# A hand-ordered plan for attention and channel mix on one core: every step in another place

## The chip, the core and the metric

The kernel runs on one core of a Trainium2 chip. A core has a matrix engine (TensorE, "PE" in the profile, with its weight loads as "PEld"), a vector engine (VectorE, "DVE"), a scalar engine (ScalarE, "ACT"), a general engine (GpSimd, "POOL") and a queue engine (SyncE, "SP"). Each runs its own list of instructions in order; they meet through semaphores. DMA transfers are issued from the lists of SyncE, ScalarE and GpSimd and share 16 DMA engines. Matmul results go to PSUM, which has eight banks. The metric is device time in microseconds (us) of one execution.

## The reference

Eight batches of 576 tokens, eight heads of 64 columns, 32 memory slots a head. Attention first squeezes keys and values into the memory slots, then each token attends to the 32 slots; a channel mix follows on the 512 columns.

```
a    = softmax over tokens of phi                  # per batch, head
k_m  = a^T k ;  v_m = a^T v                        # 32 x 64 per head
attn = softmax(q k_m^T / 8) over the 32 slots
x    = attn v_m                                    # heads side by side: 576 x 512
xk   = mu_k x + (1 - mu_k) x_prev ;  xr likewise with mu_r    # x_prev: the token before
out  = sigmoid(xr w_r) * (relu(xk w_k)^2 w_v)
```

The inputs and the output are float32.

## The kernel before

The work is cut into several hundred small steps. A text, `PLAN`, names them one after the other, and the loop at the kernel's end (L801) runs through its words and issues the instructions of each. Since every engine takes its instructions in that order, `PLAN` is the order of the work on each engine, and a semaphore wait on one engine holds all that stands behind it there.

A word is `who:name`, with marks behind it. `/a` has the step's copy or scaling done by ScalarE, `/d` by VectorE. `@` and digits name the PSUM banks that its matmuls write. A step whose matmuls are read later comes as two or three words: the first issues the matmuls, the next the reading. `who` is:

- a batch number, for attention: `exp` (exponentials of phi, L292), `z` (their sums and a reciprocal, L322 and L326), `k`, `v`, `kv` (slot means of keys and values, L312), `nk`, `nv` (dividing them), `tk` (turning the key means), `q0`, `q1` (turning q on VectorE, L381), `s` (scores, L395), `es` (their exponentials), `fe`, `fs`, `fo` (sums over the slots, by a turn, a reduction and a turn back on VectorE, L435 to L447), `w0`, `w1` (dividing, L458), `vt`, `vm` (turning the value means and mixing them with mu), `d` (differences of neighbouring tokens' weights). `G` and `E` multiply the value means into w_k and w_r and copy the products (L492, L498), `D` subtracts two of these (L501).
- `cN`, batch N's keys: `c2:5` is the sixth block of 128 columns of the hidden layer. Two matmuls with the weights, then a copy of that bank into a second one, then four matmuls with the differences, two in each (L617, L621, L625). `r` is the relu, `s` the square.
- `g` and `t`, the gate; `x` a gathering of leftover rows; `o` the product with w_v, with the gate applied and the store issued (L760, L771, L745).
- `p`, a load issued on GpSimd's queue: `p:v:1` is v of batch 1 (L181), `p:wk:2-4` a block of 256 columns of w_k (L208), `p:phi:4` L177.
- `b:NxM`, N matmuls of M times 64 columns on zeros whose result nobody reads (L259). A first group, `WARM = (10, 8)`, stands ahead of the plan.
- `w:03`, the store of a finished output tile that was held (the tiles in `HOLD`).

Batch 0 goes another way than the rest. It starts before most weights are there, so its q comes in two parts (`q:0a`, `q:0b`), as do its v, its scores (`s0`, `s1`), exponentials (`es00` to `es11`), denominators (`l`, `r`) and weights (`y`). `h` divides its key means. It mixes value means into whole token rows (`nk0`, `nr0` and so on here scale by mu, `mk`, `mr` are matmuls, L355, and `uk`, `ur` copies, L545) and then runs plain matmuls with w_k and w_r (`c0:3b`, L599; `g:00`, L666). `a` behind a key block is the first 256 tokens, `b` the other 320; `mk0` prepares `a`, `mk1` `b`. In batch 0's outputs `o:02a` and `o:02b` are column halves.

Loads on GpSimd's queue wait for two things: the buffer that they fill (two of each kind, so that batch 2 follows batch 0), and the load eight places ahead of them, whose semaphore they use again.

The stores of the last tile are cut in two: `o:71a` (352 columns) goes on ScalarE's queue and `o:71b` (160 columns) on SyncE's (`WHOLE`).

## Time and profile before

| | us |
|---|---|
| median of 3 runs | 189.69 |
| lowest, highest run | 189.14, 190.38 |
| span of the profiled execution | 187.8 |
| TensorE busy | 181.2 |
| VectorE busy | 153.9 |
| ScalarE busy | 151.9 |

The profile comes from one execution. Its page gives the span from first to last instruction, 187.8 us, and no other time for it; the median run stands 1.9 us above. "Busy" is the time in which an engine ran at least one instruction. TensorE's matmuls overlap and their ends are modelled, so the distance between the starts of two groups tells more of what a group costs than its own length. The "granted clock" is the share of full speed that the matrix engine was given. A DMA share over 1 means that several packets were in each DMA engine at once.

### The profile page before, as it was taken

How to read it: one execution, taken by the hardware profiler on the slowest of the kernel's cores; microseconds unless marked ns; L12 is line 12 of the kernel's file. 1: busy time of each engine (PE TensorE's matmuls, PEld its weight loads, DVE VectorE, ACT ScalarE, POOL GpSimd, SP SyncE). 2: the span in 40 equal slices, each digit the busy share in tenths (PEclk: the TensorE clock that was granted, in tenths of full speed). 3: DMA queues.
4: the chain of work that ended last, by engine and by line, in shares of the span. 5: the costliest groups of instructions: out<-in, count | busy, mean ns of one | idle time of the engine just before them, and what ended most of it. 6: DMA issues, size and time to landing. Idle time of an engine off the chain costs nothing.

```text
span 187.8 us, 6010 instructions
## 1 busy us (share of the span) xinstructions
PE 181.2 (96%) x2483; PEld 103.2 (55%) x2483; DVE 153.9 (82%) x328; ACT 151.9 (81%) x368; POOL 30.2 (16%) x46
## 2 busy tenths in 40 slices
PE   7979999999999999999999999999999999999992
PEld 2544566677644575556544655556545653465441
DVE  2334574899989999999999899999989999889441
ACT  2537889889999999999999889958999678775900
POOL 5943531060303040140032000000000010000000
PEclk9999999999999999999999999999999999999999
DMA  5999999999999999899989995114202224242054
GB/s 188 280 203 220 251 207 205 266 208 234 308 208 210 275 292 255 160 220 224 223 163 237 234 278 197 28 59 113 56 0 59 58 59 113 56 108 63 0 139 140
DMA packets 24923, 31.91 MB, mean 170 GB/s; under 512 B 1880, under 2 KB 19040, under 8 KB 24896
## 3 DMA queue, kind: packets, MB, share of 16 engines
q0 software_dynamic: 17936, 20.45, 59.0%
q1 hardware_dynamic: 5664, 9.00, 17.2%
q10 hardware_dynamic: 1296, 2.08, 3.3%
q8 instruction: 19, 0.31, 0.7%
q14 instruction: 8, 0.07, 0.1%
HBM read 38.28 MB, written 9.44 MB: 254 GB/s over the span
## 4 chain that ended last, share of the span: by engine, by line
PE 90%; DMA 4%; DVE 2%; issue 1%; ACT 1%; POOL 0%; POOLq 0%; DVEq 0%
PE pv L760 34%; PE pk L617 8%; PE pk L625 8%; PE pb L625 7%; PE gps L492 6%; PE pk L599 4%; DMA q<-in_q_dram 4%; PE pr L687 3%; PE pb L687 3%; PE pr L679 3%; PE kvps L312 3%; PE pr L709 2%; PE pr L666 2%; PE scps L395 2%; PE idle L259 1%
## 5 line engine op out<-in xcount | busy, mean ns | idle before, releaser
L760 PE MATMUL pv<-wv,sq 128*128 128x512 bf16 (+3 forms) x296 | 60.5, 350 | 0.0
L760 PEld LDWEIGHTS <-sq 128*128 128x128 bf16 x296 | 27.7, 98 | 24.9 <-issue 2.8
L498 ACT CAST G<-gps 128x512 bf16<-128x512 f32 x67 | 36.2, 629 | 1.2 <-PE gps L492 1.2
L771 DVE SCALAR_TENSOR_TENSOR o<-sg,pv 128x512 f32<-128x512 f32 (+3 forms) x41 | 24.9, 613 | 7.5 <-PE pv L760 5.1
L625 PEld LDWEIGHTS <-G 128*128 128x128 bf16 x224 | 21.4, 98 | 8.5 <-issue 0.7
L583 ACT ACTIVATE rl<-pk 128x288 bf16<-128x288 f32 (+2 forms) x49 | 20.0, 420 | 4.5 <-PE pk L625 3.9
L625 PE MATMUL pk<-diff,G 128*128 128x288 bf16 x112 | 22.9, 286 | 0.0
L625 PE MATMUL pb<-diff,G 128*128 128x288 bf16 x112 | 22.9, 286 | 0.0
L617 PE MATMUL pk<-atn,G 128*128 128x288 bf16 x112 | 20.8, 287 | 0.0
L621 ACT COPY pb<-pk 128x288 f32<-128x288 f32 x41 | 16.4, 410 | 5.1 <-PE pk L617 3.5
L591 DVE TENSOR_TENSOR sq<-rl 128x576 bf16<-128x576 bf16 (+2 forms) x46 | 18.3, 420 | 1.0 <-ACT rl L583 0.5
L583 ACT ACTIVATE rl<-pb 128x288 bf16<-128x288 f32 x40 | 16.2, 427 | 2.2 <-PE pb L625 1.8
L589 ACT ACTIVATE sq<-rl 128x576 bf16<-128x576 bf16 (+2 forms) x26 | 15.7, 624 | 0.5 <-DVE rl L585 0.4
L501 DVE TENSOR_TENSOR G<-G 128x1024 bf16<-128x1024 bf16 x21 | 14.3, 679 | 1.3 <-ACT G L498 1.3
L458 DVE TENSOR_TENSOR atn<-e,lz 128x576 bf16<-128x576 bf16 (+2 forms) x18 | 12.1, 683 | 3.5 <-ACT lz L430 3.5
L617 PEld LDWEIGHTS <-G 128*128 128x128 bf16 x112 | 10.2, 98 | 6.6 <-issue 1.5
L656 ACT ACTIVATE sg<-pr 128x512 f32<-128x512 f32 x22 | 13.0, 618 | 0.7 <-PE pr L687 0.6
L259 PE MATMUL idle<-zeros 128*128 128x512 bf16 (+3 forms) x47 | 12.2, 408 | 1.0 <-DVE zeros L187 1.0
L381 DVE STREAM_TRANSPOSE qT<-q 128x576 uint32<-128x576 uint32 (+2 forms) x16 | 12.1, 765 | 1.2 <-DMA q<-in_q_dram 1.2
L585 DVE TENSOR_SCALAR rl<-pk 128x288 bf16<-128x288 f32 (+2 forms) x23 | 10.1, 449 | 2.8 <-PE pk L599 2.6
L498 DVE CAST G<-gps 128x512 bf16<-128x512 f32 x17 | 11.3, 679 | 0.2 <-PE gps L492 0.2
L292 ACT ACTIVATE em<-ph 128x1152 bf16<-128x1152 f32 (+1 forms) x9 | 9.9, 1095 | 1.6 <-DMA ph<-in_phi_dram 1.6
(101 smaller groups left out, 283.7 us busy)
## 6 DMA issues: line engine op xcount, KB each, us to landing
out_dram<-o SPq DMA_DIRECT2D x46, 128.0 KB, 2.4
ph<-in_phi_dram POOLq DMA_DIRECT2D x7, 576.0 KB, 12.2
q<-in_q_dram POOLq DMA_DIRECT2D x7, 576.0 KB, 13.6
kv<-in_k_dram POOLq DMA_DIRECT2D x7, 576.0 KB, 14.2
kv<-in_v_dram POOLq DMA_DIRECT2D x7, 576.0 KB, 15.0
out_dram<-o SPq DMA_DIRECT2D x6, 256.0 KB, 6.5
out_dram<-o SPq DMA_DIRECT2D x20, 64.0 KB, 2.5
k0f<-in_k_dram ACTq DMA_DIRECT2D x2, 576.0 KB, 5.8
```

The source lines that it names most:

```text
L259: nc.tensor.matmul(ps.rearrange("p (a b) -> p a b", b=64), lhsT=zeros, rhs=zeros[:, :64].unsqueeze(1).to_broadcast([128, blocks, 64]), sta ...
L498: return lambda: copier()(g_tile()[:, v, c, GCOLS[i]], st["gps", v, i][c])
L501: return lambda: nc.vector.tensor_sub(g_tile()[:, 1, :, GCOLS[i]], g_tile()[:, 2, :, GCOLS[i]], g_tile()[:, 0, :, GCOLS[i]])
L583: nc.scalar.activation(rl, ps, AF.Relu, scale=HALF ** 0.5)
L589: nc.scalar.activation(dst, rl, AF.Square)
L591: nc.vector.tensor_mul(dst, rl, rl)
L617: nc.tensor.matmul(pa, lhsT=st["G"][:, 2, c, f], rhs=st["at"][:, c, :NP], start=c == 0, stop=False, skip_group_check=True)
L621: copier()(pb, pa)
L625: nc.tensor.matmul(ps, lhsT=st["G"][:, v, c, f], rhs=st["d"][:, kind, c], start=False, stop=c == 1, skip_group_check=True)
L656: nc.scalar.activation(gated[name], ps, AF.Tanh, scale=0.5)
L760: nc.tensor.matmul(pv[:, cols], lhsT=squares, rhs=wv_sb[:, fi, cols], start=(fi == 0), stop=(fi == NF - 1))
L771: nc.vector.scalar_tensor_tensor(o[:, cols], in0=gated[name][:, cols], scalar=1.0, in1=pv[:, cols], op0=AL.add, op1=AL.mult)
```

## The change

`PLAN` alone changes. All steps of real work are in both plans, each once; their order, the engine marks and the banks differ. The places that the later sections speak of:

- The unread matmuls. Behind `WARM`, the old plan has 37 in seven words ahead of the first key block. The new one has 22 in seventeen words, most of them ahead of `0:kg1`, and one more (`b:1x8`) ahead of `g:00`.
- The start of batch 0. `0:z`'s reciprocal and the two `0:h` stand ahead of `0:q0`, and both `0:h` are on VectorE. `0:vg1` and `0:vg0` stand ahead of the denominators `0:l11` and `0:l01`. `0:mk0` and `0:mr0` and the first 256 tokens' key blocks come first, where the old plan begins with `0:mk1` and the other 320 tokens.
- Loads. `p:wk:2-4` goes ahead of `p:wk:4-8`; `p:wv:0-2` ahead of `p:phi:2`; from there on q, k, v and phi of the later batches are in another order.
- `o:03b` stands ahead of `1:v`.
- The held stores `w:03`, `w:02`, `w:13`, `w:00`, `w:01` stand in the key stages of batches 1 and 2 instead of 3 and 4.
- The sums of batch 3 (`3:fe 3:fs 3:fo 3:w0`) stand close together on VectorE.
- The last words are `o:71b` and then `o:71a`.

```
 PLAN = [
-    "p:q:0b 0:c01/d 0:exp1 p:v:0h 0:c00/a 0:exp0 b:11x6@5 0:mub@0 0:mub 0:kg0@12 0:c10/d 0:c11/a b:2x8@5 0:kg1",
-    "0:z@0 0:q0 0:z 0:h1/a p:v:0g 0:h0/a b:7x7@5 0:tk@3 0:tk 0:q1 b:2x6@5 0:s0@1204 0:s1@3567 0:es00 0:es10",
-    "0:l00@1 0:l00 b:1x4@0 0:l10@2 0:l10 0:r00 0:y00 0:r10 0:y10 0:es01 0:es11 b:9x8@0 0:l11@4 0:l01@7 0:l01",
-    "0:r01 0:vg1@65 0:vg0 0:y01 0:nk0 0:l11 0:nk1 0:r11 0:y11 b:5x7@0 0:mk1@7321 0:uk11/a p:wk:4-8 0:mu@4",
-    "p:wk:2-4 0:uk10/d c0:3b@0 c0:4b@2 0:tb p:wk:0-2 c0:1b@1 c0:1b/d 0:nr1 c0:3b/a c0:3b/d p:phi:1 c0:0b@7 0:nr0",
...
-    "1:fe 1:fs g:02@4 g:03@6 g:01 g:03 o:02b@0 g:00@6 x:0/a c0:6a/d g:02 1:v@23 o:03b@5 1:fo 1:nv/a 1:vt@3 1:vm",
...
-    "c2:2 r:200/a r:201/a c2:4/a@1 3:tk r:220/d 4:q0 3:s@4035 r:221/a 3:es1 3:es0 p:v:4 c2:3@6 c2:3/d@7 s:20/d",
-    "c2:4 r:240/a c2:1@3 c2:7@5 c2:3 c2:1/a@0 4:q1 r:230/a g:20@4 s:22/d c2:7/a@2 r:231/a c2:1 r:211/a c2:5@6",
-    "r:241/a c2:5/a@7 c2:7 r:271/a 2:D2 3:fe 3:fs s:23/a r:270/a o:11@0 r:210/a o:11 g:20/a@1 c2:5 c2:6@3 3:vt@5",
...
-    "r:330/d s:31/d c3:0@4 c3:4 s:32/a s:35/a s:36/d g:30@6 o:23 w:03 w:00 g:31@7 c3:0/a@1 g:31/d@0 p:k:6 c3:0",
...
-    "s:76/a g:71/d@5 g:71 r:720/d s:72/d t:700 t:710 g:e3 t:711 r:730/d s:73/d x:7/a o:70@1 o:70 o:73@2 o:e3@1",
-    "o:73 t:701 o:e3 o:72@2 o:72 o:71a@0 o:71a o:71b@4 o:71b",
+    "0:exp0 b:1x4@3 0:mu@6 0:mu b:1x2@4 0:exp1 b:1x2@5 b:1x4@2 0:mub@2 b:2x8@7 0:z@1 b:1x8@5 0:c11/a b:2x8@4 b:1x8@4",
+    "0:c00/d 0:c01/d b:1x4@0 b:1x8@5 b:1x8@3 b:1x2@0 0:c10/d 0:z 0:kg0@34 0:kg1 b:2x8@0 b:2x8@5 0:h0/d 0:h1/d b:1x8@7",
+    "0:q0 0:tk@4 0:tk 0:s0@5310 0:es00 0:l00@6 0:es10 b:1x4@7 0:l00 0:r00 0:l10@5 0:l10 0:r10 p:q:0b 0:q1 p:v:0h",
+    "0:mub 0:s1@2763 0:es01 0:es11 p:v:0g 0:vg1@04 0:vg0 0:l11@3 0:l11 0:l01@6 0:l01 0:r01 0:r11 0:y00 0:y10 0:nk1",
+    "0:nk0 0:mk0@2157 b:2x8@3 0:nr1 0:nr0 0:uk01/d 0:y01 0:y11 0:mr0@7310 0:ur01/d p:wk:2-4 0:uk00/a c0:2a@6 c0:3a@4",
+    "c0:3a/d c0:3a/d p:wk:4-8 0:ur00/a 0:mk1@2573 p:wk:0-2 0:uk10/a p:phi:1 p:q:1 0:uk11/d c0:7a@0 c0:7a/a c0:7a/a",
...
+    "1:tk@4 1:tk 1:s@6521 1:es0 1:es1 1:fe 1:fs b:1x8@4 g:00@4 g:00 g:03@7 g:03 g:02@5 g:02 o:02b@2 g:01@6 o:03b@4",
+    "1:fo 1:w1 1:v@15 o:03b 1:w0 o:00b@3 o:02b g:01 x:0/a 1:nv/a 1:vt@7 1:vt/d 1:vm o:00b o:01b@6 o:01b 1:G00@45",
...
+    "c1:7@5 c1:4@0 r:101/a s:12/d r:100/d o:03a w:03 c1:7/a@1 c1:5 c1:7 r:170/d r:150/d c1:4/a@7 r:151/d 1:D2 3:exp",
...
+    "o:12@1 o:12 2:Es10/a 2:E000/a g:10/a@0 g:10 w:02 w:13 w:00 3:z@2 p:phi:4 4:exp 2:D0 w:01 t:100 t:101 2:G01@14",
...
+    "c2:0/a@4 3:tk@1 3:tk 2:D2 o:10@2 c2:0 r:200/a r:201/a o:10 c2:2 r:221/d 4:q1 c2:4@6 r:220/a c2:4/a@2 3:s@7451",
+    "3:es1 c2:3@0 c2:3/d@3 c2:4 r:241/d 3:es0 p:q:5 p:v:5 s:20/d 3:fe s:22/d 3:fs 4:q0 p:q:6 p:k:5 r:240/a s:24/d",
+    "3:fo 3:w0 c2:1@5 c2:1/a@2 c2:7@1 c2:7/a@6 c2:3 r:231/a r:230/a 4:z@7 c2:5@4 c2:5/a@3 c2:1 r:210/a c2:7 r:270/a",
...
+    "s:73/d s:71/a s:77/d s:70/a x:7/d o:62@2 o:62 g:70@1 g:70/d@4 o:70@7 g:70 t:701 g:71 t:700 o:70 o:73@3 g:e3@6",
+    "o:e3@2 t:710 t:711 o:73 g:e3 o:e3 o:72@1 o:72 o:71b@3 o:71b o:71a@5 o:71a",
 ]
```

## The prediction

> **What bounds the kernel now.** I read the page first, then stages, TensorE in order of time, and the loads that its first 40 us wait for.

> ```profile
> span 187.8 us, 6010 instructions
> PE 181.2 (96%) x2483; PEld 103.2 (55%) x2483; DVE 153.9 (82%) x328; ACT 151.9 (81%) x368; POOL 30.2 (16%) x46
> ```

> TensorE is busy for all but 6.6 us of the span. The stages (stretch, length, busy time of PE, PEld, DVE, ACT, POOL with instruction counts, granted clock, DMA share, GB/s) say where it isn't, and what runs beside it. The first two rows are of the same stretch, the second counts the unread matmuls alone:

> ```profile
> 12.00:15.40 3.40, 2.99 (x77) 1.47 (x75) 1.29 (x3) 2.48 (x9) 1.49 (x3) 1.00 1.22 206
> ```

> ```profile
> 12.00:15.40 3.40, 2.02 (x10) 0.87 (x9) 1.00 1.22 206
> ```

> ```profile
> 45.00:60.00 15.00, 15.00 (x237) 8.69 (x234) 14.25 (x33) 14.76 (x36) 2.98 (x4) 1.00 1.18 247
> 60.00:80.00 20.00, 20.00 (x326) 11.66 (x325) 19.57 (x37) 19.94 (x53) 2.98 (x4) 1.00 1.08 243
> ```

> From 45 us on TensorE has no free time, with VectorE and ScalarE close behind it. Ahead of that much of its work is filler (2.02 of 2.99 us in the first stretch). So a new order can gain in three places only: before the dense stretch starts, in small bubbles inside it, and after its end. TensorE's timeline (start, length, instruction) gives the edges:

> ```profile
> 0.99 4.38 PE L259 MATMUL idle<-zeros 128*128 128x512 bf16 x10 [0.99 <-DVE zeros L187]
> ```

> ```profile
> 19.75 3.54 PE L599 MATMUL pk<-x0T,wk 128*128 128x320 bf16 x24 [0.45 <-DVE x0T L545]
> ```

> ```profile
> 33.78 1.04 PE L760 MATMUL pv<-wv,sq 128*128 128x256 bf16 x8
> 34.66 1.03 PE L666 MATMUL pr<-wr,x0T 128*128 128x512 bf16 x4
> 35.61 0.75 PE L312 MATMUL kvps<-kv,em 64*32 64x64 bf16 x72
> ```

> The first key matmul starts at 19.75 us; the row at 35.61 is the step 1:v, batch 1's v means. Its data come over GpSimd's queue (issue row, then the DMA view of that moment, whose last number is us from issue to landing):

> ```profile
> 17.38 0.75 POOL L181 DMA_DIRECT2D kv<-in_v_dram  x1 [1.42 <-DMA wk<-in_moe_w_k_dram]
> ```

> ```profile
> kv<-in_v_dram POOLq DMA_DIRECT2D x1, 576.0 KB, 18.1
> ```

> 17.38 + 18.1 = 35.5 us: 1:v starts 0.1 us after its data are there. No wait shows, but nothing may come earlier either. The DMA engines are full throughout (share over 1), so this load is paced by what is queued ahead of it.

> **The start.** The chain that ended last begins with the first half of q (start, length, work):

> ```profile
> 3.08 7.02 DMA q<-in_q_dram
> 10.12 0.84 DVE qT L381
> 11.06 0.63 ACT kbd L337 x2
> ```

> ```profile
> 12.06 0.30 DVE kmT L365
> 12.40 0.53 PE scps L395 x30
> ```

> q lands at 10.10 in both plans, since GpSimd's queue begins alike. In the old plan VectorE turns q (0:q0) ahead of the reciprocal 0:z, so the key means are normalised (kbd, 11.06) only after the turn, and the scores wait until 12.40. The new plan puts 0:z and both normalisations (0:h0/d, 0:h1/d) on VectorE ahead of 0:q0; when the turn ends, at 10.12 + 0.84 = 10.96, only the 0.30 copy kmT is left. Scores start at about 11.35: 1.05 us earlier. The next stop is v's second half of batch 0, for 0:vg0, which now stands ahead of the denominators 0:l11 and 0:l01:

> ```profile
> 15.08 0.88 POOL L208 DMA_DIRECT2D wv<-in_moe_w_v_dram  x1 [1.22 <-DMA kv<-in_v_dram]
> ```

> ```profile
> 16.06 0.38 PE L420 MATMUL zps<-e,sumh 128*128 128x256 bf16 x2
> ```

> GpSimd's row shows that half landing just before 15.08, so the denominators come at about 15.2 instead of 16.06, 0.85 us earlier, and with them the first key: 18.9 us. It may be up to 1 us less, because the new plan starts with the first 256 tokens (0:mk0, c0:2a), which need the first half of the attention weights alone (0:y00, 0:y10, not 0:y01, 0:y11); I take 18.9, the later one. The column block of wk that these need is moved to the front of the wk loads (p:wk:2-4 ahead of p:wk:4-8), so that it doesn't bound them.

> **What the start is worth.** Counted word by word, everything that TensorE does ahead of 1:v in the old plan is ahead of it in the new one, and one thing more: o:03b, 8 matmuls of 256 columns, which cost 34.66 - 33.78 = 0.88 us. From first key to 1:v the old plan takes 35.61 - 19.75 = 15.86 us. The new one adds 0.88, a filler of 512 columns (about 0.2, an eighth of the 1.73 us of a value step below), and swaps mixing steps across the first key, 0:mk0 and 0:mr0 going ahead of it and 0:mk1 coming behind (two tile groups leave and one comes, of which I count no gain). It would be at 1:v at 18.9 + 15.86 + 1.1 = 35.85 with the late key, at 34.9 with the early one; about 35.5 between. The load says 35.5 too, and can't be beaten: GpSimd's order up to p:v:1 has the same loads. TensorE works in order, so o:00b, 1:vt and 1:G00 behind 1:v wait with it, whatever was won before. So 1:v comes 0.1 us earlier, with 0.88 us less left to do: a gain of 0.95 us, of which the late key would take 0.35.

> **The middle.** Behind 1:v both plans hold the same matmuls. Changes between full-array and tiled matmuls, which leave small gaps, number 27 groups behind the first key in the old plan and 26 in the new one, the one missing having moved ahead of it: no term. By the /a and /d marks some fifteen short copies (0:h, 0:ur, vt, nv) go from ScalarE to VectorE and a few back; TensorE's work hides them while neither engine falls behind. I cost the middle at nothing; a bubble that is new is a rival below.

> **The end.** The last output tile's columns are stored in two parts, 352 and 160 wide, and their order is swapped: the wide one is now last.

> ```profile
> L771 DVE SCALAR_TENSOR_TENSOR o<-sg,pv 128x352 f32<-128x352 f32 x1 | 0.5, 521 | 0.6 <-PE pv L760 0.6
> ```

> ```profile
> L771 DVE SCALAR_TENSOR_TENSOR o<-sg,pv 128x160 f32<-128x160 f32 x1 | 0.3, 320 | 0.0
> ```

> ```profile
> out_dram<-o ACTq DMA_DIRECT2D x1, 176.0 KB, 2.3
> ```

> ```profile
> out_dram<-o SPq DMA_DIRECT2D x1, 80.0 KB, 2.3
> ```

> After TensorE's last matmul the product takes 521 instead of 320 ns; both stores land 2.3 us after issue, and ScalarE's queue is as free as SyncE's. Loss: 0.2 us. A gain is excluded, since the wider product follows the same last matmul; if the wide product were hidden in part, the loss would go towards 0. I take +0.2, the rows' own difference.

> **The sum.** -0.95 + 0.2 = -0.75 us on the profiled span of 187.8, so 187.1. The span is the only time that the page gives; the median of the runs, 189.69, lies 1.9 above it, and I carry that over: **188.9 us**.

> **Rivals.** *Bubbles go too.* TensorE's weight loads stood idle for want of instructions, by the waits:

> ```profile
> PEld L492 <- issue: 4.4, 15, 0.4
> ```

> Nearly all of this lay under running matmuls (TensorE is 15.00 of 15.00 us busy), and the new plan has as many such groups in as long runs; if a quarter of the 4.4 us is exposed and all of it vanishes, 1.1 us, the time is 187.8. Chance 0.08.

> *The clock falls.* The first ten matmuls took 4.38 us, 0.43 each; eight of the same width later take 1.73 us, 0.22 each (the value step below). The granted clock reads 1.00 with TensorE 2.99 of 3.40 us busy; the new plan leaves 0.1 to 0.5 us of the 2.02 us of fillers there, so it would be busy for some 1.3 of 3.4 us, and no row shows that the clock stands it. If it drops for one phase as long as the first, 4.4 us, half of that, 2.2 us, is lost, 1:v comes at 37.7 instead of 35.5, and the time is 191.1. [...] The trace is silent on it. Chance 0.12.

> *Stores push the loads.* This one ends slower. Five finished tiles of 256 KB (03, 02, 13, 00, 01), which the old plan holds back to batch 3's and 4's key stages, are now stored beside batch 1's and 2's, ahead of 4:kv, where the stage rows have the DMA share over 1.

> ```profile
> q1 hardware_dynamic: 5664, 9.00, 17.2%
> ```

> ```profile
> 58.27 0.75 POOL L181 DMA_DIRECT2D kv<-in_k_dram  x1
> ```

> ```profile
> kv<-in_k_dram POOLq DMA_DIRECT2D x1, 576.0 KB, 13.1
> ```

> ```profile
> 75.90 0.80 PE L312 MATMUL kvps<-kv,em 64*32 64x128 bf16 x72
> ```

> The stores' and fast loads' queue takes 17.2% of 187.8 us for 9.00 MB: 3.6 us a MB. 1.31 MB cost 4.7 us. k of batch 4 lands at 58.27 + 13.1 = 71.4 and is used by 4:kv at 75.90, in the new plan at 75.0; it may slip by 3.6 us, and by one load of phi more, which now comes behind it. At 4.7 it is about on time. If a store among loads costs twice that, 9.4 us, TensorE waits at 4:kv for some 4 us: 193. [...] Chance 0.08.

> *VectorE falls behind.* The new plan puts batch 3's normalisation (3:fe, 3:fs, 3:fo, 3:w0) in one run between c2:3's copy and 3:vm, with 4:q0, relus and squares.

> ```profile
> L458 DVE TENSOR_TENSOR atn<-e,lz 128x576 bf16<-128x576 bf16 x14 | 10.3, 749 | 0.0
> L447 DVE STREAM_TRANSPOSE lz<-se 128x1152 f32<-128x1152 f32 x7 | 9.6, 1375 | 0.0
> L441 DVE TENSOR_REDUCE se<-eT 128x36 f32<-128x1152 bf16 x7 | 9.4, 1347 | 0.1
> ...
> L435 DVE STREAM_TRANSPOSE eT<-e 128x576 uint32<-128x576 uint32 x7 | 5.4, 770 | 1.4 <-ACT e L409 1.4
> ```

> ```profile
> 45.37 0.24 PE pk L617 x2
> ...
> 71.04 1.75 PE pv L760 x8
> ...
> 74.02 0.43 PE pr L687 x2
> ```

> The four are 4.2 us, with the eight smaller steps between them about 7.8 (estimate). TensorE has 14 key pairs of 0.24, six gate pairs of 0.43, one value step of 1.75 and 4:kv of 0.80 in the same run: 8.5 us. So VectorE may enter it 0.7 us late; each further us is lost, and a wait of 4:q1 for its load starts it. At 2 us lost: 190.9. Chance 0.22.

> The plan does what it says in any case: it names every step's place.

> **Chances.** My forecast keeps 0.50. Runs of this kernel spread from 189.14 to 190.38, so about 1% (1.9 us) can be told from no change. Faster than 187.8 is half of the first rival and a sliver of the forecast: 0.06. Slower than 191.6 is the stores' 0.08 and a quarter of the clock's and VectorE's 0.34, at more than the price set: 0.16. The rest, 0.78, is within 1%. The range runs from the first rival's 187.8 to a little over the clock's and VectorE's prices: 187.7 to 191.4; the stores' 193 is left out.

> **What would show it.** Right: scores at about 11.4 us, first key between 17.8 and 18.9, clock 1.00 throughout, 1:v at 35.5 behind a short wait of TensorE, TensorE full from there to about 183.2, 0.5 us of product and 2.3 us of store after it. Wrong: 1:v clearly ahead of 35.5 (the load wasn't fixed), or TensorE idle on VectorE between 65 and 80 us, on DMA at 4:kv, or a clock under 1.00 between 12 and 25 us.

## The result and the profile after

The new plan is slower: 191.98 us (189.59 to 193.44, 20 runs) beside 189.32 us (189.14 to 190.38, 20 runs) for the old one. The ratio is 1.0095, interval 1.0075 to 1.0115. It leaves out runs over 1.5% above the fastest; here these are the ones that lost most, so the medians (+1.4%) say more. The forecast was 188.9, range 187.7 to 191.4.

The page of the profiled execution (190.74 us; TensorE's busy time, and the clock row in 40 slices):

```profile
span 188.9 us, 5999 instructions
PE 180.4 (95%) x2469; PEld 102.7 (54%) x2469; DVE 157.9 (84%) x342; ACT 149.5 (79%) x354; POOL 30.1 (16%) x46
PEclk9995899999999999999999999999999999999998
```

The fourth and fifth slice (14 to 24 us) aren't at full clock. The stretches quoted before the result, of the new plan; the second row counts the unread matmuls alone:

```profile
12.00:15.40 3.40, 2.15 (x96) 1.32 (x99) 1.61 (x4) 2.75 (x10) 1.90 (x3) 0.78 1.31 202
45.00:60.00 15.00, 15.00 (x227) 9.14 (x226) 14.73 (x35) 14.98 (x37) 5.08 (x7) 1.00 1.19 235
60.00:80.00 20.00, 19.99 (x332) 11.87 (x330) 19.40 (x41) 18.94 (x50) 4.51 (x6) 1.00 1.15 277
```

```profile
12.00:15.40 3.40, 0.27 (x1) 0.78 1.31 202
```

From 45 us on nothing has changed: TensorE is full, at clock 1.00. All that was lost was lost before. TensorE's timeline of the new plan (start, length, instruction, wait in brackets):

```profile
10.98 0.38 PE L393 MATMUL scps<-qT,kmT 32*32 32x160 bf16 x32 [0.54 <-DVE kmT L363]
...
15.13 0.66 PE L310 MATMUL kvps<-kv,em 64*32 64x64 bf16 x34 [0.76 <-issue]
15.72 0.61 PE L418 MATMUL zps<-e,sumh 128*128 128x256 bf16 x2
...
18.75 1.89 PE L597 MATMUL pk<-x0T,wk 128*128 128x256 bf16 x8
20.57 0.52 PE L353 MATMUL mxps<-atn,vm 32*64 32x256 bf16 x32
...
29.04 1.00 PE L310 MATMUL kvps<-kv,em 64*32 64x64 bf16 x72
30.82 0.28 PE L359 MATMUL ktps<-identity,kbd 128*128 128x128 bf16 x2 [0.79 <-DVE kbd L337]
31.49 0.49 PE L393 MATMUL scps<-qT,kmT 32*32 32x288 bf16 x32 [0.38 <-DVE kmT L363]
31.91 0.39 PE L257 MATMUL idle<-zeros 128*128 128x512 bf16 x1
32.36 2.75 PE L664 MATMUL pr<-wr,x0T 128*128 128x512 bf16 x12
...
37.65 0.75 PE L310 MATMUL kvps<-kv,em 64*32 64x64 bf16 x72
...
40.23 0.41 PE L490 MATMUL gps<-wk,vM 64*32 64x512 bf16 x8
```

The rows are the scores (10.98), a wait amid v's means (15.13), the second denominators (15.72), the first key (18.75), 1:k (29.04), the gates (32.36), 1:v (37.65) and the first G product (40.23). Scores and first key come about when I said. But 1:v is 2.04 us later than the old plan's 35.61. Behind it the new plan has 151.25 us left where the old one has 187.8 - 35.61 = 152.2, the 0.9 us of o:03b and a little of the tail. 2.04 - 0.95 is the 1.1 us of span by which the profiled executions differ. Three things between 10 and 38 us are new: a stretch at half clock, a wait of 0.76 us for "issue" at 15.13 (TensorE waited for nothing else that the profile shows), and 1.17 us of waits on VectorE (0.79 and 0.38), with 0.45 us of unread matmul (31.91 to 32.36) right behind them.

### The profile page after: what moved, and what is told of

Its sections match the earlier page's. It is cut to its first block, busy times and chain, and to the rows that moved or that the text cites. A ratio compares the mean times of both kernels' runs of the same rounds, so it can differ in the third digit from the quotient of the medians.

```text
span 188.9 us, 5999 instructions
## 1 busy us (share of the span) xinstructions
PE 180.4 (95%) x2469; PEld 102.7 (54%) x2469; DVE 157.9 (84%) x342; ACT 149.5 (79%) x354; POOL 30.1 (16%) x46
## 2 busy tenths in 40 slices
DMA packets 24939, 31.91 MB, mean 169 GB/s; under 512 B 1896, under 2 KB 19056, under 8 KB 24912
## 4 chain that ended last, share of the span: by engine, by line
PE 86%; DMA 5%; DVE 4%; issue 2%; POOL 2%; POOLq 0%; DVEq 0%
PE pv L758 34%; PE pk L615 8%; PE pk L623 7%; PE pb L623 7%; PE gps L490 6%; DMA kv<-in_v_dram 5%; PE pr L677 3%; PE pr L685 3%; PE pb L685 3%; PE kvps L310 3%; PE pk L597 3%; PE pr L707 2%; PE pr L664 2%; PE scps L393 2%; PE mxps L353 1%
## 5 line engine op out<-in xcount | busy, mean ns | idle before, releaser
L758 PEld LDWEIGHTS <-sq 128*128 128x128 bf16 x296 | 27.8, 98 | 25.7 <-issue 1.7
L496 ACT CAST G<-gps 128x512 bf16<-128x512 f32 x67 | 35.2, 626 | 2.0 <-PE gps L490 1.7
L615 PE MATMUL pk<-atn,G 128*128 128x288 bf16 x112 | 19.7, 286 | 0.0
L587 ACT ACTIVATE sq<-rl 128x576 bf16<-128x576 bf16 (+2 forms) x28 | 16.4, 616 | 0.3
L581 ACT ACTIVATE rl<-pb 128x288 bf16<-128x288 f32 x39 | 15.4, 432 | 0.7 <-PE pb L623 0.6
L654 ACT ACTIVATE sg<-pb 128x512 f32<-128x512 f32 x14 | 8.8, 630 | 4.1 <-PE pb L685 4.1
L583 DVE TENSOR_SCALAR rl<-pk 128x288 bf16<-128x288 f32 (+2 forms) x22 | 9.6, 452 | 2.8 <-PE pk L597 2.1
L496 DVE CAST G<-gps 128x512 bf16<-128x512 f32 x17 | 11.2, 686 | 0.3 <-PE gps L490 0.3
L407 ACT ACTIVATE e<-scps 128x288 bf16<-128x288 f32 x28 | 9.3, 415 | 2.4 <-PE scps L393 2.3
## 6 DMA issues: line engine op xcount, KB each, us to landing
ph<-in_phi_dram POOLq DMA_DIRECT2D x7, 576.0 KB, 14.6
q<-in_q_dram POOLq DMA_DIRECT2D x7, 576.0 KB, 14.1
kv<-in_k_dram POOLq DMA_DIRECT2D x7, 576.0 KB, 16.2
kv<-in_v_dram POOLq DMA_DIRECT2D x7, 576.0 KB, 12.2
k0f<-in_k_dram ACTq DMA_DIRECT2D x2, 576.0 KB, 5.5
```

The costliest lines, as they stand in the source:

```text
L496: return lambda: copier()(g_tile()[:, v, c, GCOLS[i]], st["gps", v, i][c])
L581: nc.scalar.activation(rl, ps, AF.Relu, scale=HALF ** 0.5)
L587: nc.scalar.activation(dst, rl, AF.Square)
L615: nc.tensor.matmul(pa, lhsT=st["G"][:, 2, c, f], rhs=st["at"][:, c, :NP], start=c == 0, stop=False, skip_group_check=True)
L654: nc.scalar.activation(gated[name], ps, AF.Tanh, scale=0.5)
L758: nc.tensor.matmul(pv[:, cols], lhsT=squares, rhs=wv_sb[:, fi, cols], start=(fi == 0), stop=(fi == NF - 1))
```

## The experiments

Two theories at first. The clock: too little unread matmul work is left, TensorE falls to half speed for a while. The queue: VectorE takes batch 1's kbd and kmT too late, and TensorE stands between 1:k and the gates. The rival to both was something in the middle or in the loads. A plan's words are given as short diffs; "after" stands for the new plan, "before" for the old.

**Fillers, gate order, and both (e1_filled, e2_gates, e3_both).** e1 puts 16 unread matmuls of 512 columns more into after and widens one (the expectation counts that one too); e2 moves gate groups ahead of and between batch 1's steps; e3 does both.

```
e1  0:q0 0:tk@4 [+b:3x8@7] 0:tk 0:s0@5310 [+b:3x8@7] 0:es00 ... b:1x4@7 -> b:1x8@7 0:l00
    0:vg1@04 [+b:3x8@1] 0:vg0 [+b:1x8@1] 0:l11@3 ... 0:l01 [+b:3x8@1] 0:r01
    b:2x8@3 -> b:4x8@3 0:nr1 ... 0:mr0@7310 [+b:1x8@6] 0:ur01/d
e2  1:k@71 1:nk/d [+g:00@0]
-   1:tk@4 1:tk 1:s@6521 ... 1:fs b:1x8@4 g:00@4 g:00 g:03@7 g:03
+   1:tk@4 1:tk g:03@3 1:s@6521 ... 1:fs g:00 g:03
```

> The new plan with 17 more unread matmuls of 512 columns in TensorE's gaps between 10 and 19 us, about as dense as in the old plan; nothing else moves. Theory of the clock (the thinner fillers let the granted clock fall to a half at 13.9 us, which cost about 1 us of first keys and, by its chance phase, the spread of the runs): granted clock 1.00 from the start's release on, first key at about 18.7 us and the eight first key matmuls in 0.9 instead of 1.8 us, 1:v at 36.7 instead of 37.65, span 187.9 instead of 188.9, and runs within 1 us of each other. Rival (the order itself is slower, the clock is a side show): 1:v stays at 37.4 or later and the span above 188.6.

> The new plan with the gate matmuls g:00 and g:03 moved up between 1:k, 1:tk and 1:s, and the one late filler ahead of g:00 taken out; the thin fillers stay. Theory of VectorE's queue (TensorE idles 1.9 us between 1:k and g:00 because 1:nk and 1:tk stand behind 1:q0, 1:q1 and two copies on VectorE): the gates fill that wait as soon as w_r is there at 30.3 us, 1:v comes 1.5 us earlier, about 36.1, span about 187.4 where the clock falls as it did in the new plan, runs still spread over 3 us. Rival (w_r or the v load sets that place, not VectorE): 1:v moves by less than 0.5 us.

> Both edits at once. If clock and VectorE's queue are the two things that my forecast missed, 1:v stands at the landing of its load, 35.8 us, with TensorE waiting for it, span 187.1 and time 188.9 as forecast, 0.3% under the kernel before. If 1:v comes clearly ahead of 35.8 the load was no bound; if it comes after 36.3 without a wait for the load, something third is late.

Times: 191.79, 191.84 and 191.41 us against 189.33 (ratios 1.0128, 1.0122, 1.0112). In e1 and e3 the clock fell in one run of eight only, and the spread shrank (190.95 to 192.75), but the time stayed: the first key came at 20.84 and 19.81 us, since the blocks stood ahead of steps that others waited for; in e1's profiled run the clock's release was also late, at 5.82 us. In e2's profiled run the trace's clock records have the release at 13.78 us only (3.65 in after's): eight unread matmuls of 512 columns took 3.25 us from 8.71 on, where after's take 1.84. From 1:k to 1:v e2 took 7.77 us, after 8.61: VectorE's queue and the unread matmul that e2 leaves out cost 0.84 us there together. In e2 and e3 new waits came in, 0.84 us for ScalarE's exponentials and 1.00 us ahead of the first G product. None of the three settles the price of the clock, since each brings a loss of its own.

**Thin fillers in the old plan (e4_old_thin).**

```
before: -b:9x8@0   b:5x7@0 -> b:2x8@0
```

> The old plan with 12 of its unread matmuls taken out (the 9 ahead of 0:l11, and 2 instead of 5 ahead of 0:mk1), so that the stretch from 12 to 18 us is as thin as in the new plan. Theory of the clock: the granted clock falls to a half there, the first keys run at half speed, the time grows by 1 to 2.2 us and the runs spread. Rival (the thinness does nothing, it is the new order): clock 1.00, time as before within 0.3%.

191.49 us, ratio 1.0104 (1.0065 to 1.0144). The old plan loses 1% by this alone. Two neighbouring stretches of its profile:

```profile
12.57:15.99 3.42, 1.17 (x52) 0.65 (x37) 1.15 (x3) 3.09 (x12) 1.62 (x2) 1.00 1.25 204
15.99:19.40 3.41, 3.41 (x109) 1.66 (x108) 1.28 (x4) 1.49 (x4) 1.46 (x2) 0.50 1.34 263
```

TensorE worked 1.17 of 3.42 us, and the next 3.41 us ran at 0.50. After's clock goes the same way, for two such stretches:

```profile
10.47:13.89 3.42, 2.02 (x103) 1.24 (x104) 2.31 (x6) 2.33 (x8) 1.93 (x3) 1.00 1.25 203
13.89:17.30 3.41, 2.24 (x55) 1.06 (x55) 1.69 (x6) 2.04 (x9) 1.64 (x2) 0.50 1.30 202
17.30:20.71 3.41, 3.41 (x34) 1.50 (x40) 2.14 (x7) 1.45 (x5) 0.88 (x1) 0.50 1.22 290
```

After's clock records have the release at 3.65 us, the fall to 0.50 at 13.89 (10.24 us on, three times 3.41) and the rise to 1.00 at 20.71 (6.83 more, twice 3.41); in all traces the changes lie at such multiples. So the question is what tells the stretches that are followed by half speed from the others.

**Time or array (e7_small).** Same count, same columns, but a sixteenth of the array.

```
before, in keep_busy: + w = 32 if n in (9, 5) else 128     (the words b:9x8, b:5x7)
  matmul(ps[:w], lhsT=zeros[:w, :w], rhs=zeros[:w, :64] repeated)
```

> The old plan with the nine unread matmuls of 512 columns behind the second denominators and the five of 448 ahead of the first mixes done on 32 rows and 32 columns of the array in place of 128 and 128: same count, same columns, same time on TensorE, a sixteenth of the array. Counting in stretches of 3.41 us from the clock's release, every stretch that was followed by half speed had at most 1,824 columns, weighed by the part of the array that they use, and every one that was followed by full speed at least 2,600; by TensorE's busy time they overlap (0.59 and 0.66 of a stretch were followed by half speed, 0.64 and 0.67 by full). If the used part of the array counts: the stretch around 14 to 17 us falls to some 1,500 to 2,300, the clock falls to half for one stretch of 3.41 us in most runs, mean clock 0.991 or 0.982, time 190.5 to 191.5 like the plan in which the same blocks were left out (191.5). If busy time counts: clock 1.0, time as before, 189.3.

191.09 us, ratio 1.0061; its ten runs had a mean clock of 0.97 to 1.0, and the two at 1.0 took 189.27 and 189.54, the old plan's time. In its profile:

```profile
13.22:16.64 3.42, 3.32 (x75) 1.37 (x47) 0.89 (x2) 2.87 (x12) 1.47 (x2) 1.00 1.29 202
16.64:20.05 3.41, 3.41 (x106) 1.67 (x89) 1.28 (x4) 1.37 (x4) 1.04 (x3) 0.50 1.27 285
```

TensorE was busy 3.32 of 3.42 us, with no gap to speak of, and the clock fell to 0.50. Busy time doesn't tell the stretches apart: 2.28 us (e1) and 2.61 (the old plan) were followed by full speed. What e7 changes is the used part of the array. I weigh each matmul's columns by rows x columns of its tile over 128 x 128 and sum them over each stretch of 3.41 us from the release, a matmul in the stretch in which it starts. About 8,100 fit, an estimate from the old plan's trace, where full-array matmuls of 512 columns start 0.216 us apart at full speed:

| kernel, stretch from | TensorE busy, us | weighed columns | next stretch |
|---|---|---|---|
| e4, 12.57 | 1.17 | 1,408 | half |
| after, 10.47 | 2.02 | 1,760 | half |
| e7, 13.22 | 3.32 | 1,928 | half |
| e6, 20.14 | 1.22 | 2,240 | half |
| e10, 27.52 | 2.17 | 2,338 | half |
| e2, 17.19 | 2.34 | 2,600 | full |
| e1, 12.65 | 2.28 | 2,720 | full |
| before, 8.58 | 2.61 | 4,082 | full |

**Narrow early blocks, and everything at once (e5_packet, e6_best, e8_no_packet).** In after, e1, e2 and e3 TensorE waited for "issue" right behind its 222nd matmul, whatever that was (0.76, 1.13, 0.61 and 0.85 us). e5 makes the early blocks narrow and many to move this edge; e8 has 10 unread matmuls of 512 columns more, fewer than e1 and placed where TensorE waits (the expectations say 12, a miscount), and another gate order; e6 has both.

```
e5  b:2x8@7 -> b:16x1@7   b:2x8@4 -> b:16x1@4   0:z [+b:26x1@0] 0:kg0@34
e8  0:tk@4 [+b:2x8@7] 0:tk 0:s0 [+b:3x8@7] ... 0:vg0 [+b:2x8@1] ... 0:l01 [+b:2x8@1] ... b:2x8@3 -> b:3x8@3
    1:nk/d [+g:00@0] 1:tk g:03@3 1:s ... g:00 g:03 g:02@4 g:02 ... 1:v@14; 1:w0 behind 1:vm
```

> The new plan with three of its early unread blocks cut narrower: two of 2 matmuls of 512 columns become 16 of 64 each, and 26 of 64 are added ahead of batch 0's k means, 54 matmuls more ahead of its v means. In the new plan and in all three variants of it so far TensorE stood still for 0.6 to 1.1 us, waiting for nothing that the profile shows, right after its 222nd matmul, which was the 2nd, the 32nd, the 2nd or the 2nd of a group of v means. Theory (instructions come in portions, and this one is late because the roughly 110 matmuls ahead of it are tiny): the portion's edge stays at matmul 222, which is now the 16th of the second scores; it is asked for about 0.9 us earlier, so the gap there is under 0.4 us and the v means run through. Then the first key comes 0.6 to 0.8 us earlier against the same start (from the first scores to the first key 7.8 us in the new plan, here about 7.1 if the clock does the same). Rival (the gap is the price of the wait for v's landing in front of it): it stays in the v means, 0.6 to 1.1 us. The clock is left as it is: some windows of half speed, time 190.5 to 192.

> The new plan with all that the theories name mended: the narrow early blocks of the run before, 12 more unread matmuls of 512 columns placed where TensorE waits anyway in batch 0 (2 and 3 around the first scores, 2 and 2 around the denominators, one between the mixes), and of batch 1 the gate groups g:00, g:03 and g:02 begun ahead of and between the turned k and the scores, on banks that are free, with the fold's last turn 1:w0 behind 1:vm. If lost clock, late instructions and VectorE's queue between 1:k and the gates are the whole of the loss: clock 1.0 from its release in most runs, first key at 17.8 to 18.6 us, 1:k at 27.2 to 28, 1:v at 35 to 35.8, where the landing of its load at 35.5 shows for the first time, time 188.2 to 189.0, under the old plan's. If the middle of the new plan is slower than I read it (after 1:v it was 0.85 us shorter), the time stays over 189.5 although 1:v is as early as the old plan's 35.6.

> The run e6_best without the narrow early blocks. Theory (instructions in portions): 0.6 to 1.1 us of gap at matmul 222, in the v means, first key and 1:v 0.5 to 0.9 us later than there, unless 1:v then waits for its load in both; time 0.2 to 0.7 us over e6_best. Rival (the early blocks do nothing): the two agree within 0.2 us.

Times 194.03, 195.43 and 191.43 us. The edge stayed at matmul 222, as the theory said, now amid the scores; but the gap didn't shrink, a second one came, and the clock fell in every run of e5 and e6 (means of 0.973 to 0.991). TensorE's waits for issue in e6_best:

```profile
16.21 0.30 PE L393 MATMUL scps<-qT,kmT 32*32 32x128 bf16 x21 [0.98 <-issue]
...
22.41 0.31 PE L353 MATMUL mxps<-atn,vm 32*64 32x256 bf16 x6 [2.19 <-issue]
```

The second stands behind matmul 350, 128 further on; e5 has the same two (0.74 and 1.15 us). From the start of matmul 223 to that of 351 it takes 22.41 - 16.21 = 6.20 us, and 6.20 us again in e5, e8, e10, f2 and f3, wherever that second wait shows (in e8 and e10 the profile puts its 0.20 us down to a VectorE copy). My reading, an estimate from the 128 matmuls and the 6.20 us: instructions reach TensorE in portions of 128 matmuls, and where it waits for one like this, the portion comes 6.2 us behind the one before. The DMA records go with it: the queue that the page calls "instruction" moves packets of 16 KB (19 of them in after, 0.31 MB), and in e6_best two of them start at 13.88 and 19.94 us, with none between; the waits end 2.3 and 2.5 us behind these starts. In after the packet starts at 12.86 us and the wait ends 2.3 us later. In the old plan it starts at 12.76, but TensorE comes to matmul 223 only at 16.56 and doesn't wait. Cutting blocks narrower was the wrong cure: e5 and e6 have two waits for issue where after has one. In e8 the clock held in all five runs (0.999 to 1.0), and still the time was 191.43: there TensorE waited 0.70 us for wr's load at g:00 and 0.90 us for 1:vm.

**The clock alone, and VectorE's order (e10_clock, e9_vector, e11_tail).** e10 is after with e8's 10 unread matmuls and nothing else. e9 adds g:00 between 1:tk and 1:s and puts 1:w0, 1:w1 and two output products behind 1:vm on VectorE. e11 is e9 with `o:71a` ahead of `o:71b`.

> The new plan with the 12 light unread blocks of the run e8_no_packet (clock held), and batch 1's steps put so that VectorE reaches the v means' mix 1:vm sooner: the gate group g:00 between the turned k and the scores, all others behind the scores (nothing that waits for wr or for ScalarE stands ahead of the scores), and on VectorE 1:vm straight behind the fold's last turn lz, with the two products of attention 1:w0, 1:w1 and the output products o:03b, o:02b behind it, as the old plan has them. Theory (batch 1's fold on VectorE, 7 us from the scores to 1:vm, sets when the dense part starts, and 1:v has room): scores at 30.6 to 31.2 us, lz done at 36.5 to 37.1, the first G matmul at 37.5 to 38.4 (40.2 in the new plan, 38.2 in the old one), span 186.3 to 187.2, time 188.0 to 189.0. By my prediction's step (1:v is held by its load at 35.5): 1:v at 35.5 and everything behind it as in the new plan, G at 38.1. Rival (the middle itself is slower than it looks): time 189.5 or more with G before 38.5.

> The new plan with the 12 light unread blocks alone. If the clock were the whole loss: clock 1.0 in nearly all runs, time 189.0 or less. If VectorE's fold of batch 1 is the second part: TensorE idle 1.1 us between 1:k and the gates as in the new plan, first G matmul at 39.2 to 39.8, time 189.4 to 190.2, 1.0 to 1.5 us over e9_vector.

> The run e9_vector with the old order of the last two stores (352 columns first, 160 columns last). My prediction's last step: 0.2 us less than e9_vector, the time of the shorter product. What the two traces show (from TensorE's end to the end of the span 3.66 us in the new plan and 3.77 in the old one): 0.1 us more than e9_vector, or no difference.

e10: 190.20 us (ratio 1.0033, 1.0011 to 1.0055) beside 189.53. Seven of its twelve runs held the clock (mean 0.996 or more) and took 189.31 to 190.29; those at 0.991 or less 191.14 and more. The old plan was timed again beside each version: after is 2.7 us over its median, e10 0.7, so 10 unread matmuls won back 2.0 us; the seven runs at full clock have a median of 189.98, 0.45 over. e9 took 192.26 us. It failed by stalls of my own, 1.08 us in the G products, whose banks the moved output products still held, and 0.78 us behind that for a copy of G on VectorE. e11 took 192.54: the old order of the last stores is no better.

**VectorE's queue and the start (f1_k_early, f2_start, f3_start_only, f4_early_means).** f1 is e10 with 1:k ahead of the last two key groups, which then cover kbd and kmT as g:01 and c0:4a do in the old plan; it also leaves out b:1x8. f2 is f1 with the old kind of start; f3 has the start without f1's part; f4 mends f2's start.

```
f1  c0:3b@6 1:z@2 1:k@73 c0:0b@0   1:q0 1:q1 1:z 1:nk/d c0:4b/a 1:tk@2 c0:4a@1 1:tk 0:ur11/d ...
    1:s@6273 ... (no b:1x8) g:00@4 g:00 g:03@0 ... 1:v@12 ... 1:vm 1:vt/d 1:w0 o:00b
f2  f1 + 0:exp0 b:11x6@5 0:mu@6 0:mu 0:exp1 0:mub@2 0:z@1 0:c11/a 0:c00/d 0:c01/d 0:c10/d 0:z
         0:kg0@34 0:kg1 b:7x8@0 0:h0/d 0:h1/d ... b:3x8@1 0:vg1@04     (other early blocks left out)
f4  f2, 0:mu@6 behind 0:kg1, 0:mu behind 0:h1/d, b:7x8@0 -> b:4x8@0
```

> The run e10_clock (the new plan with 12 light unread blocks) with batch 1's k means 1:k moved ahead of the last two key groups of batch 0 (c0:0b, c0:4a), which then lie between 1:k and the scores and cover VectorE's kbd and kmT as they did in the old plan; on VectorE 1:z and 1:nk stand ahead of the copies 0:ur11, and the attention product 1:w0 behind 1:vm; no unread block between scores and gates. Its load of k lands at 27.3 us, so 1:k is at 27.3 to 27.8 us (28.45 in e10_clock), kbd 0.9 us later, scores at 29.6 to 30.3 (30.9), TensorE without a wait from 1:k to the first G matmul, that at 38.0 to 38.9 (41.1 in e10_clock's profile, at half speed for 3.4 us of it; 40.2 in the new plan, 38.2 in the old). Theory (clock and VectorE's queue between 1:k and the gates are the whole loss): with the new plan's own 148.7 us from there to the end the span is 186.7 to 187.6, clock 1.0 in nearly every run, time 188.4 to 189.3. Rival (a third cause behind the first G matmul): G at 38 to 39 and the time 189.8 or more.

> The run f1_k_early with the old plan's kind of start: the 11 unread matmuls of 512 columns in one piece right behind the first ten, the small ones that stood between the first real steps left out, the casts and batch 0's k means straight behind them, 7 of 512 columns between these and the turned k, and 3 ahead of the v means, under the gap at matmul 222. Theory (third cause: the new plan's start has more to do on TensorE ahead of the first scores, so it comes later by as much as the clock's release does, 3.6 to 13.8 us in the runs so far, and the stretch of scores, v means and gap starves the clock at some phases): release at 3.4 to 6.9 us, first scores at 11.2 to 11.8 us whatever the release, gap at matmul 222 ending at 14.6 to 15.2, first key at 17.8 to 18.7, clock 1.0 in nearly every run, first G matmul at 37.4 to 38.4, span 186.6 to 187.6, time 188.3 to 189.4 with a spread as small as the old plan's. Rival (the rest of the new plan is what costs): the same start and G at about 38, but 189.8 or more.

> The new plan with the light unread blocks and the old kind of start, but batch 1's k means, gates and fold as the new plan has them. If VectorE's queue between 1:k and the gates is worth its idle time: TensorE idle 1.1 to 1.2 us there and 0.45 us of unread matmul, first G matmul 0.6 to 1.2 us later than in f2_start, time 0.6 to 1.2 us over it, about the old plan's. If it is hidden by something that ends later anyway: within 0.3 us of f2_start.

> The run f2_start with one flaw of its own mended: there VectorE's casts of k stood behind the copy 0:mu, which waited for TensorE until 8.09 us (the cast at 8.18, in the old plan at 6.54), so the k means ran at 8.84 to 10.0 and matmul 94 came at 9.84 (8.83 in the new plan). 0:mu now stands behind the k means, and 4 unread matmuls of 512 columns, not 7, follow them. Theory (with the clock held and VectorE's queue cleared, the first key is set by the supply of instructions, about 6 us from matmul 94 to matmul 222, and the time goes with the first key): matmul 94 at 8.3 to 9.0, matmul 222 at 14.4 to 15.1, first key at 18.0 to 18.8 (19.55 in f2_start), time 0.7 to 1.4 us under f2_start's 189.9, so 188.5 to 189.2, a little under the old plan. Rival (the first key doesn't set the time; 1:k's load at 27.3 or VectorE behind it does): first key earlier, time within 0.4 us of f2_start.

f1: 190.94 us; its profiled run had its release at 6.20 us, the first key at 20.86, and a stretch of 1,728 weighed columns around the wait for issue; half speed again. Its six runs below 190.6, all at clock 1.0, have a median of 190.05, 0.3 over the old plan's 189.72, where e10's are 0.45 over: with the new kind of start, the mended order on VectorE shows no gain that could be told from the noise. f2: 189.92 us (1.002, 1.0005 to 1.0035), mean clock 0.996 or more in every run, all within 189.44 to 190.72. f3: 190.49. With the old kind of start, clearing VectorE's queue is worth 0.57 us, about half of the 1.17 us that TensorE waits there in f3. f4: 189.46 us (189.03 to 190.07), ratio 1.0002 (0.9989 to 1.0014): the old plan's time. I had expected 188.5 to 189.2. TensorE's timeline of f4:

```profile
15.84 0.44 PE L310 MATMUL kvps<-kv,em 64*32 64x64 bf16 x36 [0.89 <-DMA kv<-in_v_dram]
...
19.18 1.05 PE L597 MATMUL pk<-x0T,wk 128*128 128x256 bf16 x8
...
28.15 0.75 PE L310 MATMUL kvps<-kv,em 64*32 64x64 bf16 x72 [0.43 <-DMA kv<-in_k_dram]
...
36.43 0.75 PE L310 MATMUL kvps<-kv,em 64*32 64x64 bf16 x72
```

With clock, queue and issue out of the way it waits for loads: v of batch 0, then k of batch 1. Another 0.87 us ahead of the first scores go to VectorE's kmT, behind its turn of q, which begins at 10.51 us, when q has landed. But this run took 190.04, one of the two slowest of its twelve, and its loads came late (k of batch 1 at 28.1 us, in after at 27.7, in the old plan at 26.8), so it may show more waiting than the median run has. No version beat the old plan.

## Why the prediction was wrong

**The start** held. Scores at 10.98 us (forecast 11.35), first key at 18.75 (17.8 to 18.9). The denominators came at 15.72 instead of 15.2, behind the wait for issue. That the key was on time all the same is partly luck: from the denominators to the key the old plan takes 3.69 us and the new one 3.03, though at half clock. I had put the shorter way of the first 256 tokens at up to 1 us and left it out of the 18.9.

**What the start is worth** is the step that failed. I let TensorE run from first key to 1:v without any loss and only the load v:1 stop it at 35.5. From first key to 1:v I had 15.86 + 1.1 = 16.96 us; it took 37.65 - 18.75 = 18.90. The load landed at 35.8, near the forecast, but TensorE came 1.8 us behind it. In no version of the new plan did it wait for that load, and none has 1:v under 36 us (f4 is nearest, at 36.43 behind a landing at 36.2). Missing from that step were the clock and the waits on VectorE; the wait for "issue", missing too, cost its 0.76 us ahead of the key. The first eight key matmuls cost 20.57 - 18.75 = 1.82 us; in e8, at full clock, 1.0:

```profile
18.46 1.05 PE L597 MATMUL pk<-x0T,wk 128*128 128x256 bf16 x8
19.44 0.48 PE L353 MATMUL mxps<-atn,vm 32*64 32x256 bf16 x32
```

**The clock rival** was right in what fell (the clock, to 0.50) and where (13.89 to 20.71 us), and I gave it 0.12. Its price, 2.2 us and 191.1, is near the 191.98 and the 2.0 us that e10 wins back. That 1:v came at 37.65 where the rival had 37.7 is luck: about 1 us of it is clock, and 1.17 us are the waits on VectorE. The rival's single phase of 4.4 us was two stretches of 3.41 in the trace. I named the stretch (TensorE busy 1.3 of 3.4 us; it was 2.15, with 0.27 of unread matmul), but had no row for a threshold and took the silence for safety. Nor were short waits a sign of safety: behind the first matmul none was over 0.8 us in after, and in e7 TensorE was busy 97% of the stretch. The changes of the clock lie at multiples of 3.41 us from the release, and the release lies at another time in each trace (3.65 us in after's, 5.82 in e1's, 13.78 in e2's), so which steps share a stretch changes from run to run. That this makes the spread is an estimate from the mean clocks: after's runs with 0.991 took 189.59 and 190.75 us, those with 0.973 took 192.47 to 192.95. A stretch at half speed takes 0.5 x 3.41 us off some 185 us, 0.009 of the mean, so the first have one and the others three, about 1.2 us for each further one.

**VectorE** was a rival in the wrong place. At batch 3 TensorE didn't wait (19.99 of 20 us busy from 60 to 80). The new marks and order made VectorE late at batch 1. The stretches 25 to 30 us of before and of after:

```profile
25.00:30.00 5.00, 5.00 (x149) 3.85 (x136) 2.77 (x7) 4.42 (x16) 0.85 (x3) 1.00 1.31 202
```

```profile
25.00:30.00 5.00, 4.94 (x140) 3.49 (x137) 4.97 (x15) 4.78 (x13) 1.49 (x2) 1.00 1.32 204
```

VectorE has 4.97 us of work there instead of 2.77. "TensorE's work hides them while neither engine falls behind" was my sentence for these copies; one engine did, and of the two groups that had covered kbd and kmT, g:01 now lay behind the scores and c0:4a ahead of 1:k.

**The middle** at nothing held. **The stores** pushed no load that TensorE waited for: from 40 us on it has no wait at all. **The end** cost nothing where I had 0.2 us: the last product is the wide one, as said,

```profile
185.45 0.52 DVE L769 SCALAR_TENSOR_TENSOR o<-sg,pv 128x352 f32<-128x352 f32 x1 [0.83 <-PE pv L758]
```

but from its end, 185.97, to the end of the span it is 2.9 us. In the old plan the last two products end at 183.76 + 0.82 = 184.58, 3.2 us ahead of the end:

```profile
183.76 0.82 DVE L771 SCALAR_TENSOR_TENSOR o<-sg,pv 128x352 f32<-128x352 f32 x2 [0.56 <-PE pv L760]
```

The longer product and the shorter rest cancel (e9 and e11 differ by 0.28 us the other way, within their intervals), so the term should have been 0, not +0.2.

**The sum**, then. Over the old plan's median beside which each was timed, after is 2.7 us, e10 0.7, f3 0.9, f2 0.3 and f4 0.1. So the clock is 2.0 us (after to e10); the old kind of start lost 0.2 as I first built it (e10 to f3) and gave 0.2 once mended (f2 to f4); VectorE's queue at batch 1 is 0.6 (f3 to f2). Only the clock's part is far clear of noise. VectorE's is barely clear of it and shows with the old kind of start alone (f1 has no such gain), and the two changes of the start lie within the noise. f4 is then the old plan's time. The 0.75 us that I had counted as gain isn't there. That the loads of v and k take it is read from the one trace of f4 and not shown; another order of loads was not tried.

## What to carry to other kernels

Unread matmuls are part of the schedule's cost: before thinning them, add up the array's used columns in every 3.41 us, wherever the first of these stretches may begin. Here 2,338 or less were followed by half speed and 2,600 or more by full, and a stretch of e7, mostly of small tiles, had 1,928 in 3.32 busy us. Where hundreds of tiny matmuls stand together, count instructions too: here TensorE waited 0.61 to 1.60 us for issue behind its 222nd in eleven traces. And a start that is paced by loads gains nothing from an earlier first step until each engine's queue from there to the dense part has been followed.

## What was unexpected

- The clock fell behind a stretch that was busy for 3.32 of 3.42 us, mostly with small tiles (e7, 1,928 weighed columns). Of about 8,100 weighed columns, 2,338 were followed by half speed, 2,600 by full.
- The clock's release came anywhere from 3.63 to 13.78 us after the start. The mean clock of a run is counted from the release on (after's 0.979 is the mean of its records from 3.65 us), so e2's profiled run, with the latest one, shows 1.0. A mean of 1.0 is thus no proof of a full clock: one run of after (192.30 us) and two of f1 (192.42 and 192.47) have it all the same; whether their release came late, no trace shows.
- TensorE waited behind its 222nd matmul and again behind its 350th, 128 further on. Where the second wait shows, in six traces, matmul 351 started 6.20 us behind matmul 223. The waits at matmuls 222 and 350 were mostly 0.2 to 2.2 us, whatever the matmuls were; the old plan and f4 have none there.
